# Removing the closing barrier of a one-core decode kernel, and splitting its last weight load

## The chip, the cores and the metric

The kernel runs on one core of one Trainium2 chip. The metric is device time in microseconds (us) for one execution. Each timed execution also gives a span: the time from the first to the last instruction that the profiler records. The time is longer than the span, by 1.27 to 1.95 us in the runs below, and that difference turns out to matter here; below it is called "time minus span".

The kernel has five engines at its disposal: TensorE (PE in the profile; PEld is its weight load), VectorE (DVE), ScalarE (ACT), GpSimd (POOL) and SyncE (SP), which here issues the store and all loads but two of 2 KB.

## The reference, cut to what matters

One token goes through a conditioned transformer block: a modulation vector from `c`, attention against a cache of 65,536 positions, and a gated feed-forward layer. Everything is a product of a vector with a matrix that is read once, so the time is mostly the time of reading 186 MB (on the page of the kernel before, loads are 75% of the chain that ended last).

```python
mod = (silu(c) @ w_mod).reshape(c.shape[0], 6, 1, -1)          # sa, ca, ga, sb, cb, gb
h = layernorm(x) * (1 + ca) + sa
x = x + ga * attention(h, k_cache, v_cache, wq, wo)             # 32 heads, 4 kv heads
h = layernorm(x) * (1 + cb) + sb
x = x + gb * ((gelu(h @ w_gate) * (h @ w_up)) @ w_down)         # w_down is 3584 x 1024
```

The change touches the last product (`w_down`, the down projection) and what follows the output store.

## The kernel before: the parts that matter

All loads are planned in one order and issued by SP. Each goes into one of ten buffers, and SP issues it once the buffer's previous user is done.

```python
def issue_ready():
    while issued[0] < len(loads):
        j = loads[issued[0]]
        if j.prev is not None:
            if j.prev.freed is None:
                return
            SP.wait(j.prev.freed)
        sp.dma_start(j.view, j.src).then_inc(j.tok[0], 16)
        issued[0] += 1
```

A product walks over its loads in order, waits for each whole load, and then issues its matmuls. With `nblk` = 8 the down projection has 8 matmuls for each 2 KB of row per partition.

```python
def matvec(bank, jobs, rhs, ready, nblk, pick=None, first=True):
    PE.wait(*ready)
    for (jb, view, k0, nk) in jobs:
        PE.wait(jb.tok)
        for kk in range(nk):
            for j in range(nblk):
                ins = pe.matmul(bank[:, j:j + 1], ..., rhs[:, k0 + kk:k0 + kk + 1], ...)
        tok = PE.done(ins)
        release(jb, tok)
    return tok
```

The down projection comes in three loads of 2 MB and two of 512 KB. Behind it stand two small VectorE operations, a transpose on TensorE, a cast and the store. The whole program is emitted inside a block, and leaving it is a barrier: in the profile of the kernel before, that line has a drain and a semaphore instruction of each of the five engines, the last ending at 442.67 us.

```python
while b < NBF:                                  # the last 1 MB: two loads of 512 KB
    for e in range(0, UE, 2):
        jb = plan_load(wd_v[:, b, e:e + 2, :], flat(2, D), next(tail))
        j_d.append((jb, jb.view, b * UE + e, 2))
    b += 1
...
    sp.dma_start(out[0, 0].rearrange("(j p) -> j p", p=P), y_row[:, :]).then_inc(out_sem, 16)
    sp.wait_ge(out_sem, 16)

with nc.Block() as block:
    @block.sync
    def _(sp_unused):
        emit_all()                              # emits on all engines
```

## Time and profile before

| | before |
|---|---|
| time, median of 3 runs | 444.28 us |
| span of the profiled run | 442.7 us |
| moved by loads, mean rate | 186 MB, 420 GB/s |
| TensorE busy | 76% of the span |
| chain that ended last | 75% loads |

These are lines of the page of the kernel before: the span, the busy share of TensorE, the load rate in 40 equal slices of the span, the sum over all load packets, and the shares of the chain that ended last.

```profile
span 442.7 us, 16779 instructions
PE 335.0 (76%) x7849; PEld 325.2 (73%) x7849; DVE 164.8 (37%) x282; ACT 143.1 (32%) x548; POOL 3.8 (1%) x21
...
GB/s 329 429 423 426 434 431 426 429 427 421 432 429 432 426 427 437 432 429 428 434 434 430 429 429 433 431 434 429 429 434 431 432 429 428 423 424 424 427 425 177
DMA packets 15392, 186.08 MB, mean 420 GB/s; under 512 B 1536, under 2 KB 1536, under 8 KB 3840
...
DMA 75%; PE 20%; issue 2%; DVE 1%; SPq 1%; ACT 1%
```

The rate is flat, 421 to 437 GB/s, from the second slice to the last but one. Only the two ends, at 329 and 177 GB/s, are not bound by the stream, and the change is at the second end.

The timeline of the kernel before shows that end. Columns: start, duration, engine, line, operation, output and inputs, count, and in brackets the idle time before and what ended it.

```profile
436.83 2.29 PE L316 MATMUL kt_ps<-u_col,slot 128*128 128x1 bf16 x80 [3.45 <-DMA slot<-in_B_w_down_dram]
...
439.28 0.58 PE L316 MATMUL kt_ps<-u_col,slot 128*128 128x1 bf16 x16 [0.15 <-DMA slot<-in_B_w_down_dram]
439.90 0.17 DVE L664 TENSOR_TENSOR t_dn<-kt_ps,mod_sb 128x8 f32<-128x8 f32 x1 [15.91 <-PE kt_ps L316]
...
441.04 0.37 SPq L672 DMA_DIRECT2D out_dram<-y_row  x1
```

TensorE does the last 2 MB load and the first 512 KB load in one go (80 matmuls), waits 0.15 us for the last 512 KB, and has 16 matmuls left. The store is issued at 441.04 us.

The barrier is on line 676. The view of that line lists each sequencer's instructions: engine, operation, count, duration in ns (least, median, most), and first and last start in us.

```profile
L676 POOLq EVENT_SEMAPHORE  x2: 17/17/17, 442.5 to 442.6; - x2
...
L676 ACTq DRAIN  x1: 256/256/256, 407.4 to 407.4; - x1
...
L676 SPq COMPARE_BRANCH  x1: 33/33/33, 442.3 to 442.3; - x1
L676 SPq DRAIN  x1: 7/7/7, 442.5 to 442.5; - x1
L676 SPq EVENT_SEMAPHORE  x1: 17/17/17, 442.6 to 442.6; - x1
...
L676 PEldq EVENT_SEMAPHORE  x1: 51/51/51, 442.6 to 442.6; - x1
```

SP's branch, at 442.29 in the instruction records, carries the wait for the store. SP's drain, GpSimd's gather and release, and the last semaphore waits of the engines follow; the last ends at 442.67. ScalarE drained at 407.4 already.

### The profile page before, as it was taken

Reading aid. Unit: us, or ns where it says so; the run is one execution under the profiler, and the core shown is the slowest. Engines: PE = TensorE matmul, PEld = TensorE weight load, DVE = VectorE, ACT = ScalarE, POOL = GpSimd, SP = SyncE. Lnnn points to the kernel's source line nnn. Section 1 sums busy time; section 2 is a strip of 40 time slices with the busy share of each in tenths; the row PEclk is TensorE's granted clock in tenths of the full one; section 3 lists DMA queues with packets and bytes.
Section 4 is the critical chain, followed back from the end, with each engine's and each line's share of the span. In section 5 each row is a group of like instructions: output and inputs, shape, how many; then the busy total and the mean of one; then the engine's idle time right before and its main releaser. Section 6 shows DMA issues by size and latency. Waiting matters only on the chain.

```text
span 442.7 us, 16779 instructions
## 1 busy us (share of the span) xinstructions
PE 335.0 (76%) x7849; PEld 325.2 (73%) x7849; DVE 164.8 (37%) x282; ACT 143.1 (32%) x548; POOL 3.8 (1%) x21
## 2 busy tenths in 40 slices
PE   1333468898979899989899988979898974654434
PEld 1333458898979899979799987969898964654434
DVE  1000046544536445544644644554544443210000
ACT  1000013444444333634533453543343562000000
POOL 2000000000000000000000000000000000000000
PEclk9999999867788956967955996895967785555555
DMA  8999999999999999999999999999999999999994
GB/s 329 429 423 426 434 431 426 429 427 421 432 429 432 426 427 437 432 429 428 434 434 430 429 429 433 431 434 429 429 434 431 432 429 428 423 424 424 427 425 177
DMA packets 15392, 186.08 MB, mean 420 GB/s; under 512 B 1536, under 2 KB 1536, under 8 KB 3840
## 3 DMA queue, kind: packets, MB, share of 16 engines
q1 hardware_dynamic: 15328, 185.61, 98.5%
q8 instruction: 25, 0.41, 0.3%
q14 instruction: 7, 0.06, 0.0%
q10 hardware_dynamic: 32, 0.00, 0.0%
HBM read 185.60 MB, written 0.00 MB: 419 GB/s over the span
## 4 chain that ended last, share of the span: by engine, by line
DMA 75%; PE 20%; issue 2%; DVE 1%; SPq 1%; ACT 1%
DMA slot<-in_A_v_cache_dram 55%; PE kt_ps L417 9%; DMA slot<-in_A_wq_dram 8%; DMA slot<-in_B_w_up_dram 6%; DMA slot<-in_B_w_down_dram 6%; PE b L481 5%; PE sc_ps L437 3%; PE kt_ps L316 1%; SPq L212 1%; PE b L461 1%; ACT p_sb L547 1%; PE b L451 1%; DVE kt_sb L612 0%; PE b L621 0%; DVE zs L597 0%
## 5 line engine op out<-in xcount | busy, mean ns | idle before, releaser
L417 PE MATMUL kt_ps<-ident,slot 128*128 128x128 bf16 x2048 | 171.9, 252 | 4.9 <-DMA slot<-in_A_k_cache_dram 3.0
L516 DVE COPY kt_sb<-kt_ps 128x2048 bf16<-128x2048 bf16 x96 | 117.5, 1225 | 100.0 <-PE kt_ps L417 99.7
L417 PEld LDWEIGHTS kt_ps<-ident,slot 128*128 128x128 bf16 x2048 | 148.6, 114 | 6.6 <-issue 4.2
L516 ACT ACTIVATE kt_sb<-kt_ps 128x2048 bf16<-128x2048 bf16 x32 | 60.1, 1878 | 217.7 <-PE kt_ps L417 217.7
L481 PE MATMUL b<-p_sb,slot 128*128 128x8 bf16 x2048 | 71.0, 167 | 29.5 <-DMA slot<-in_A_v_cache_dram 20.9
L481 PEld LDWEIGHTS b<-p_sb,slot 128*128 128x128 bf16 x2048 | 65.1, 100 | 32.2 <-DMA slot<-in_A_v_cache_dram 22.2
L547 ACT ACTIVATE p_sb<-sc_ps,mneg 128x64 bf16<-128x64 f32 x256 | 83.6, 560 | 5.7 <-DVE mneg L542 5.7
L547 ACT ACTIVATION_READ_ACCUMULATOR p_sb<-sc_ps,mneg 128x1 f32 x256 | 77.2, 364 | 0.0
L437 PE MATMUL sc_ps<-q_buf,kt_sb 128*128 128x8 bf16 x2048 | 67.4, 167 | 0.1
L437 PEld LDWEIGHTS sc_ps<-q_buf,kt_sb 128*128 128x128 bf16 x2048 | 65.1, 100 | 0.2 <-issue 0.2
L316 PE MATMUL kt_ps<-h_col,slot 128*128 128x1 bf16 x448 | 16.2, 172 | 16.9 <-DMA slot<-in_B_w_up_dram 9.1
L316 PEld LDWEIGHTS kt_ps<-h_col,slot 128*128 128x128 bf16 x448 | 15.6, 118 | 17.6 <-DMA slot<-in_B_w_up_dram 9.4
L316 PE MATMUL sc_ps<-s_col,slot 128*128 128x1 bf16 x384 | 11.5, 165 | 15.8 <-DMA slot<-in_w_mod_dram 15.8
L535 DVE TENSOR_REDUCE m_col<-sc_ps 128x8 f32<-128x512 f32 x32 | 21.8, 681 | 4.4 <-PE sc_ps L437 4.4
L316 PEld LDWEIGHTS sc_ps<-s_col,slot 128*128 128x128 bf16 x384 | 11.0, 105 | 16.4 <-DMA slot<-in_w_mod_dram 16.4
L540 DVE TENSOR_REDUCE mg<-b 8x1 f32<-8x128 f32 x32 | 8.9, 279 | 34.4 <-PE b L451 34.4
L316 PE MATMUL sc_ps<-h_col,slot 128*128 128x1 bf16 x256 | 7.4, 165 | 12.6 <-DMA slot<-in_A_wq_dram 12.6
L316 PEld LDWEIGHTS sc_ps<-h_col,slot 128*128 128x128 bf16 x256 | 7.1, 104 | 12.9 <-DMA slot<-in_A_wq_dram 9.3
L461 PE MATMUL b<-negi,mg 8*128 8x8 f32 x64 | 15.0, 304 | 0.4 <-DVE mg L540 0.4
L461 PEld LDWEIGHTS b<-negi,mg 8*128 8x128 f32 x64 | 12.0, 233 | 2.6 <-DVE mg L540 0.6
L316 PE MATMUL kt_ps<-u_col,slot 128*128 128x1 bf16 x224 | 6.6, 165 | 9.6 <-DMA slot<-in_B_w_down_dram 9.6
L316 PEld LDWEIGHTS kt_ps<-u_col,slot 128*128 128x128 bf16 x224 | 6.3, 104 | 9.9 <-DMA slot<-in_B_w_down_dram 6.8
(74 smaller groups left out, 63.2 us busy)
## 6 DMA issues: line engine op xcount, KB each, us to landing
slot<-in_A_k_cache_dram SPq DMA_DIRECT2D x32, 2048.0 KB, 29.6
slot<-in_A_v_cache_dram SPq DMA_DIRECT2D x32, 2048.0 KB, 33.2
slot<-in_w_mod_dram SPq DMA_DIRECT2D x8, 1536.0 KB, 19.0
slot<-in_A_wq_dram SPq DMA_DIRECT2D x4, 2048.0 KB, 37.0
slot<-in_A_wo_dram SPq DMA_DIRECT2D x4, 2048.0 KB, 34.7
slot<-in_B_w_gate_dram SPq DMA_DIRECT2D x4, 1792.0 KB, 39.4
slot<-in_B_w_up_dram SPq DMA_DIRECT2D x4, 1792.0 KB, 29.0
slot<-in_B_w_down_dram SPq DMA_DIRECT2D x3, 2048.0 KB, 30.4
```

The source lines that it names most:

```text
L212: sp.dma_start(j.view, j.src).then_inc(j.tok[0], 16)
L316: ins = pe.matmul(bank[:, j:j + 1], w, rhs[:, k0 + kk:k0 + kk + 1], start=first, stop=True, skip_group_check=True,)
L417: ins = pe.transpose(kt_ps[:, half * 2048 + t * P:half * 2048 + (t + 1) * P], j_k[i].view[:, b * TB + t, :], ident[:, :],)
L437: ins = pe.matmul(sc_ps[:, base + n * REP:base + (n + 1) * REP], kt_sb[:, j % 2, n, :], q_buf[:, j % SITES, :], start=True, stop=True,)
L451: ins = pe.transpose(b6[0:REP, 32:32 + P], m_col[:, j % 2, :], identf[:, :]) if emit else None
L461: ins = pe.matmul(b6[:, 256:256 + REP], mg8[:, j % 2:j % 2 + 1].to_broadcast([REP, P]), negi[:, :], start=True, stop=True,)
L481: ins = pe.matmul(b7[:, s * REP:(s + 1) * REP], j_v[j].view[:, n, :], p_sb[:, s, n, :], start=(n == 0), stop=(n == CH - 1),)
L516: ev[i % SITES][b].done(act.activation(dst, src, ACT.Copy) if E_ is AC else dve.tensor_copy(dst, src))
L535: m1[s].done(dve.tensor_reduce(m_col[:, j % 2, :].unsqueeze(2), scv, AX.X, ALU.max))
L540: m2[s].done(dve.tensor_reduce(mg8[:, j % 2:j % 2 + 1], b6[0:REP, 32:32 + P], AX.X, ALU.max))
L547: ins = act.activation(p_sb[:, s, :, h], scv[:, h, :], ACT.Exp, bias=mneg[:, j, h:h + 1], scale=scale, accum_out=z_all[:, j, h:h + 1],)
```

## The change

The intent is to save the barrier's own time behind the store, and to leave less TensorE work behind the last load to land. In this program the store depends on the last work of every other engine, so SP's wait for the store alone still comes after all of it.

```diff
-            for e in range(0, UE, 2):
-                jb = plan_load(wd_v[:, b, e:e + 2, :], flat(2, D), next(tail))
-                j_d.append((jb, jb.view, b * UE + e, 2))
+            for e, ne in ((0, 2), (2, 1), (3, 1)):
+                jb = plan_load(wd_v[:, b, e:e + ne, :], flat(ne, D), next(tail))
+                j_d.append((jb, jb.view, b * UE + e, ne))
             b += 1
@@ ...
-    with nc.Block() as block:
-        @block.sync
-        def _(sp_unused):
-            emit_all()
+    emit_all()
     return nc
```

## The prediction

> **What bounds the kernel now.** Loads. The page gives 186 MB at a mean of 420 GB/s in a span of 442.7 us, DMA engines 80% busy or more in every slice but the last, and DMA as 75% of the chain that ended last. TensorE is 76% busy. The change moves the same bytes, so only the end of the span is in play.
>
> **The tail now**, from the timeline and the instruction records (us from the span's start): 80 down-projection matmuls run from 436.83, starting 26.7 ns apart; the last starts at 438.96. TensorE then sits idle 0.15 us for the last 512 KB load (its last packet, a semaphore write, is at 438.86; TensorE resumes at 439.27). 16 matmuls end at 439.86; two DVE operations, a transpose and a cast end at 441.02. The store issues at 441.04 and SP's wait sees it at 442.29. Then come SP's branch out of the block, its drain at 442.45, GpSimd's gather and release at 442.48 and 442.56, and the other engines' last semaphore instructions, ending at 442.67.
>
> **Part 1, no closing barrier.** It removes everything after SP's wait: 442.67 - 442.31 = 0.36 us, all on the critical path. The other engines' drains go too, but ran long before (ScalarE's at 407.4, VectorE's at 440.7). The time on record is 1.6 us longer than the span, so something outside the program stays. [...] I expect no change in it.
>
> **Part 2, the split.** Packets of 4 KB take 159 ns, of 8 KB 309, of 16 KB 611: about 37 ns per KB plus some 10 ns each. Two of 2 KB should take about 170 ns where one of 4 KB took 159. Eight such pairs per engine make the last landing about 0.08 us later (estimate from those durations). [...] Against it, 8 matmuls instead of 16 remain behind the last landing: 8 x 26.7 ns = 0.21 us less. The first new load's 8 matmuls would run from 438.99 to 439.2, before the last landing is seen at about 439.35. Net gain: about 0.13 us. The extra load takes slot 5, freed when the gate product ends at about 406.5; SP would issue it at about 416.6, over 20 us before it is needed.
>
> **Sum.** 0.36 + 0.13 = 0.49 us, 0.11% of the time. Predicted 443.8 us, range 443.1 to 444.3. Chances: faster by over 2% 0.005, within 2% 0.99, slower by over 2% 0.005.
>
> **What would show it.** The span ends with SP's wait, about 1.25 us after the store's issue, near 442.2 us; TensorE's last group has 8 matmuls; 2 KB packets take near 85 ns; the store issues about 0.13 us earlier.
>
> **What would make it wrong.** [...] 2 KB packets could be slower than the larger ones suggest, so that the last load lands over 0.21 us later. Drift between runs (0.2 us in three) is as large as either part, so one pair of runs may not show the split.

## More of the kernel before

Kernels are compared only within the same rounds.

## The result

The changed kernel took 443.23 us (median of 5 runs, 443.03 to 443.25) against 444.28 us (5 runs, 444.04 to 444.35). The ratio is 0.9976, with a 95% interval of 0.9964 to 0.9988. Ratios here are the mean time of one kernel's fast runs over the mean of the other's of the same rounds, so not quite the ratio of the medians quoted. The gain is 1.05 us (0.24%). That is inside the predicted range but about twice the 0.49 us that the prediction worked out.

The lines of the changed kernel that answer to those above: the page, the timeline, and the line that now ends the program.

```profile
span 441.7 us, 16769 instructions
...
DMA packets 15537, 186.08 MB, mean 421 GB/s; under 512 B 1553, under 2 KB 1553, under 8 KB 3985
...
DMA 81%; PE 17%; issue 1%; SPq 1%; DVE 0%
```

```profile
436.37 2.86 PE L316 MATMUL kt_ps<-u_col,slot 128*128 128x1 bf16 x96 [3.02 <-DMA slot<-in_B_w_down_dram]
439.27 0.17 DVE L664 TENSOR_TENSOR t_dn<-kt_ps,mod_sb 128x8 f32<-128x8 f32 x1 [15.34 <-PE kt_ps L316]
...
440.41 0.37 SPq L672 DMA_DIRECT2D out_dram<-y_row  x1
```

```profile
L673 SPq EVENT_SEMAPHORE  x1: 17/17/17, 441.7 to 441.7; - x1
```

The program ends with SP's wait, 1.25 us after the store's issue, as predicted. In this pair of profiles the span is 0.99 us shorter: 0.36 us behind SP's wait, and 0.63 us because the store issues that much earlier (441.04 to 440.41). The prediction had 0.13 us for the second. Of the 0.63, the last landing, as TensorE sees it, accounts for 0.42 us (439.28 to 438.86 in the instruction records), and 8 matmuls fewer behind it for 0.21 us. The matmuls of the third 2 MB load already start 0.47 us earlier (436.83 to 436.37), before any load that the split touches is consumed. So the pair of profiles suggests that something other than the split moved the stream. That was the first thing to test.

### The profile page after: what moved, and what is told of

Read it like the earlier page. It is cut to its first block, busy times and chain, and to the rows that moved or that the text cites. A ratio compares the mean times of both kernels' runs of the same rounds, so it can differ in the third digit from the quotient of the medians.

```text
span 441.7 us, 16769 instructions
## 1 busy us (share of the span) xinstructions
PE 332.8 (75%) x7849; PEld 322.9 (73%) x7849; DVE 164.9 (37%) x282; ACT 143.1 (32%) x548; POOL 3.8 (1%) x21
## 4 chain that ended last, share of the span: by engine, by line
DMA 81%; PE 17%; issue 1%; SPq 1%; DVE 0%
DMA slot<-in_A_v_cache_dram 53%; DMA slot<-in_B_w_gate_dram 9%; PE kt_ps L417 9%; DMA slot<-in_A_k_cache_dram 8%; DMA slot<-in_B_w_down_dram 7%; DMA slot<-in_w_mod_dram 5%; PE b L481 4%; PE sc_ps L437 3%; PE kt_ps L316 1%; SPq L212 1%; PE b L451 0%; PE b L461 0%; DVE kt_sb L516 0%; PE b L668 0%; DVE y_row L670 0%
## 5 line engine op out<-in xcount | busy, mean ns | idle before, releaser
L417 PE MATMUL kt_ps<-ident,slot 128*128 128x128 bf16 x2048 | 170.1, 250 | 6.9 <-DMA slot<-in_A_k_cache_dram 3.2
```

The source lines that it names most:

```text
L417: ins = pe.transpose(kt_ps[:, half * 2048 + t * P:half * 2048 + (t + 1) * P], j_k[i].view[:, b * TB + t, :], ident[:, :],)
```

## The experiments

All runs are on the kernel before or on the changed kernel, with the edit named, and all returned correct results. Every call had 9 runs of the kernel before on the same chip. The table gives means; each kernel has 5 runs. "Gain" is the mean time, and the mean span, less those of the kernel before.

| run | closing barrier | last loads | time | span | time minus span | before: time minus span |
|---|---|---|---|---|---|---|
| e0 | yes | 512 + 512 KB | +0.01 | +0.02 | 1.83 | 1.84 |
| e1 | no | 512 + 512 KB | -0.95 | -0.44 | 1.34 | 1.84 |
| e2 | yes | 512 + 256 + 256 KB | -0.12 | -0.16 | 1.89 | 1.84 |
| e3 | no | 512 + 256 + 256 KB | -0.93 | -0.42 | 1.34 | 1.84 |
| f1 | no, all four others wait | 512 + 512 KB | -0.31 | -0.28 | 1.83 | 1.86 |
| f2 | no, ScalarE and GpSimd wait | 512 + 512 KB | -0.31 | -0.30 | 1.85 | 1.86 |
| f3 | no, TensorE and VectorE wait | 512 + 512 KB | -0.58 | -0.32 | 1.60 | 1.86 |
| f4 | no | 1 MB | -0.45 | +0.10 | 1.30 | 1.86 |
| g1 | no | 512 + 512 KB | -0.89 | -0.42 | 1.35 | 1.82 |
| g2 | no | 512 + 256 + 256 KB | -0.95 | -0.48 | 1.35 | 1.82 |
| g3 | no | as g2, one other load moved | +2.04 | +2.52 | 1.33 | 1.82 |
| h1 | no, ScalarE waits | 512 + 512 KB | -0.79 | -0.47 | 1.51 | 1.82 |

### The kernel before once more, and each part alone

e0 is the kernel before, unedited.

> The unchanged kernel, as a control: it gives the profile of the kernel before five more times. Theory C (chance: in the one profile shown of it a DMA engine started its loads 0.4 us late and stayed last to the end) expects spans of these runs mostly near 442.2 us, with 442.67 as an outlier. Theory S (the late engine belongs to the program as built) expects 442.6 us in all. Theory O (the barrier also costs time after the last instruction) expects time minus span near 1.6 us, against the 1.33 to 1.43 of the changed kernel's five runs.

e1 removes the barrier and keeps the loads:

```diff
-    with nc.Block() as block:
-        @block.sync
-        def _(sp_unused):
-            emit_all()
+    emit_all()
```

> No closing barrier, loads as before. The prediction's sum expects 0.36 us less than the kernel before, in the span and in the time. Theory O expects 0.36 us in the span and 0.2 us more outside it, 0.55 to 0.6 us in the time. Theory S[...] expects the last landing near 438.8 us as well and 0.9 us in the time.

e2 splits the load and keeps the block:

```diff
-            for e in range(0, UE, 2):
+            for e, ne in ((0, 2), (2, 1), (3, 1)):
```

> The split with the closing barrier kept. The prediction expects 0.13 us less, the last TensorE group 8 matmuls, the last landing 0.06 to 0.08 us later for the same start of the loads. A rival, that the split itself evens out the DMA engines, expects 0.5 us or more and the third 2 MB load of the down projection landing near 436.3 us instead of 436.8.

e3 is the changed kernel, unedited.

> Both parts, as changed, on this chip. If the parts add, its gain is that of e1 plus that of e2. The result on record says 1.05 us; the prediction says 0.49 us.

The medians were 443.95 us (e0), 442.94 (e1), 443.81 (e2) and 443.03 (e3), against 443.99 for the kernel before. The ratios were 1.0 (0.9987 to 1.0014), 0.9979 (0.9966 to 0.9993), 0.9997 (0.9983 to 1.0011) and 0.9979 (0.9965 to 0.9993). The barrier alone gives all of the gain; the split alone is not clear of noise.

The span of the first profile of before was an outlier, as theory C expected; theory S falls. In e0 the spans were 441.9 to 442.3 us, and in the 36 runs of before they were 442.0 to 442.5, with means of 442.10, 442.10, 442.38 and 442.39 on the four chips. None reached 442.67. In the first profile the last load engine to finish writes its semaphore 0.41 us behind the next one; in the profiles of e0, e1, f1, f2, f3, g1 and h1 it is 0.01 to 0.22 us. On the first three loads of the first profile that gap was already 0.32 to 0.39 us. The profile of e0 has the same program, but its last group starts 0.5 us earlier than in the first profile (438.78 against 439.28):

```profile
436.33 2.29 PE L316 MATMUL kt_ps<-u_col,slot 128*128 128x1 bf16 x80 [3.19 <-DMA slot<-in_B_w_down_dram]
...
438.78 0.58 PE L316 MATMUL kt_ps<-u_col,slot 128*128 128x1 bf16 x16 [0.16 <-DMA slot<-in_B_w_down_dram]
```

So most of the earlier landing in the first pair of profiles belonged to the run, not to the change.

With that outlier out of the way, the barrier's gain splits in two. The span loses 0.44 us in e1, near the 0.36 us of the barrier's instructions. The other half microsecond lies outside the span: time minus span falls from 1.83 us in e0 (1.75 to 1.93) to 1.34 us in e1 (1.30 to 1.37). This is theory O. The prediction had expected no change there.

### What the half microsecond outside the span is

Without the barrier, two things differ: the barrier's branch and drains are gone, and four engines reach their end before SP does (in the profile of the changed kernel GpSimd at 392.4 us, ScalarE at 407.5, TensorE at 440.1 and VectorE at 440.4, against 441.7 for SP). f1 keeps the first difference and undoes the second. It is e1 with four added waits and no barrier:

```diff
         sp.wait_ge(out_sem, 16)
+        pe.wait_ge(out_sem, 16)
+        dve.wait_ge(out_sem, 16)
+        act.wait_ge(out_sem, 16)
+        pool.wait_ge(out_sem, 16)
```

> No closing barrier, but TensorE, VectorE, ScalarE and GpSimd each wait at their end for the output store's semaphore, as SP does, so all five engines reach their end together. Theory E (in e1 about 0.5 us of the gain lies behind the last instruction, because four engines are done early and whatever ends a run on them overlaps the kernel) expects the span of e1, 441.7 us, but time minus span near 1.84 instead of 1.34, so a time near 443.5 us. Theory B (the barrier's own instructions, a branch and drains, cost that 0.5 us) expects time minus span to stay near 1.34 and the time near 443.0.

f2 adds only the waits of ScalarE and GpSimd, f3 only those of TensorE and VectorE.

> Only ScalarE and GpSimd wait for the store. If theory E holds and one of these two, which end earliest of all (407 and 391 us), sets the end, time minus span is near 1.84; if TensorE or VectorE does, it is 1.34.

> Only TensorE and VectorE wait for the store; without the wait they end about 1.2 to 1.9 us before SP. The mirror of f2: near 1.84 if one of these two sets the end, 1.34 if not, and something between if the cost adds up over the engines.

The views of f1's last lines show that it did what it was built for. All five engines end together, each with one wait and nothing else:

```profile
L673 SPq EVENT_SEMAPHORE  x1: 17/17/17, 441.9 to 441.9; - x1
L674 PEldq EVENT_SEMAPHORE  x1: 51/51/51, 441.9 to 441.9; - x1
L675 DVEq EVENT_SEMAPHORE  x1: 21/21/21, 441.9 to 441.9; - x1
L676 ACTq EVENT_SEMAPHORE  x1: 17/17/17, 441.9 to 441.9; - x1
L677 POOLq EVENT_SEMAPHORE  x1: 17/17/17, 441.9 to 441.9; - x1
```

Time minus span was 1.83 us in f1 (1.80 to 1.86), as with the barrier. Theory B, that the barrier's own instructions cost the half microsecond, falls: f1 has none of them. Theory E stands: what costs it is that engines with nothing left to do reach their end late. One thing stays untested: every engine that ends late in these runs ends with a semaphore wait of 17 to 51 ns, in the barrier as in f1, and no run gave an early engine such a wait that is already fulfilled. f2 gives the same 1.85 us (1.81 to 1.88) with two engines, and f3 1.60 us (1.56 to 1.62). The medians were 443.64, 443.68 and 443.42 us against 443.96, with ratios 0.9993 (0.9979 to 1.0006), 0.9993 (0.9979 to 1.0006) and 0.9987 (0.9973 to 1.0001).

Two engines cost as much as four, and another pair costs less, so the number of late engines alone does not explain it. Nor do the costs of the engines add up: above the 1.34 us of SP alone, f2 has 0.51 us and f3 0.26, together 0.77, and f1 with all four has 0.49. The last run, h1, lets only ScalarE wait:

```diff
         sp.wait_ge(out_sem, 16)
+        act.wait_ge(out_sem, 16)
```

> No closing barrier; of the four other engines only ScalarE waits for the store. f2 (ScalarE and GpSimd) gave time minus span 1.85 us, f3 (TensorE and VectorE) 1.60, none 1.34. If what follows the last instruction is a fixed stretch of each engine's own and the longest end counts, this run gives 1.85 if ScalarE has the long stretch, and 1.34 to 1.6 if it is GpSimd. If it is instead the number of late engines that counts, a single one should give less than the pair of f3, so below 1.6 as well; then only a value near 1.85 tells the two apart.

h1 gave 1.51 us (1.47 to 1.56), median 443.39 against 444.23 us, ratio 0.9982 (0.9969 to 0.9996). The reading that fits all these runs is that each engine has a stretch of its own behind its last instruction, by estimate from these means about 1.34 us for SP, 1.5 for ScalarE, 1.6 for the longer of TensorE and VectorE, and 1.85 for GpSimd, and that the engine that is through last counts. GpSimd's figure is by elimination, from f2 and h1 on two chips; it was not run alone, and neither were TensorE and VectorE, so this reading is argued and not shown; h1's value was, by its own expectation, not one that could decide. What fills the stretches cannot be seen, since the trace ends before them.

### The split

e2 gives -0.16 us in the span against the nine runs of before (-0.18 against e0), and e3 against e1 +0.02 us, so the split was still unclear. f4 turns its dose the other way, e1 with one load of 1 MB:

```diff
-            for e in range(0, UE, 2):
-                jb = plan_load(wd_v[:, b, e:e + 2, :], flat(2, D), next(tail))
-                j_d.append((jb, jb.view, b * UE + e, 2))
+            jb = plan_load(wd_v[:, b, :, :], flat(UE, D), next(tail))
+            j_d.append((jb, jb.view, b * UE, UE))
```

> No closing barrier, the last two 512 KB loads merged into one of 1 MB: the split's dose turned the other way. 32 matmuls remain behind the last landing instead of 16, at 26.7 ns: 0.43 us more, less at most 0.05 us for larger packets. The split's arithmetic in the prediction expects e1 plus about 0.4 us in span and time, 443.4 us; if the size of the last load hardly matters (as e3 against e1 seems to say, +0.02 us), about 443.0.

g1 and g2 are e1 and e3 again, side by side on another chip.

> The kernel of e1 a second time, for the split: e3 against e1 gave +0.02 us where e2 against e0 gave -0.16 us in the span, and f4 (1 MB) gave about +0.4 us. The arithmetic (16 matmuls at 26.7 ns behind the last landing against 8, less 0.03 us of longer stream) expects this run 0.15 to 0.2 us slower than g2 on average, and the same local stretch as before: 0.63 us from the last landing as TensorE sees it to the end of its last matmul. The rival, that the split is worth nothing without the barrier, expects the same time as g2.

> The changed kernel again, beside g1. Arithmetic: 0.15 to 0.2 us faster than g1, about 0.42 us from last landing to last matmul's end. Rival: equal to g1 within 0.05 us.

The 0.05 us for larger packets in the expectation of f4 and the 0.03 us of longer stream in that of g1 were estimates, with no source. The packet times (84 ns for 2 KB, 159 for 4 KB, 309 for 8 KB in the first two profiles) give an estimate of 0.07 us for either: 16 x 159 - 8 x 309 ns and 16 x 84 - 8 x 159 ns for each engine, taking the packets as spread evenly over 16 engines.

The profile of f4 has all 32 matmuls behind the last landing:

```profile
436.34 1.87 PE L315 MATMUL kt_ps<-u_col,slot 128*128 128x1 bf16 x64 [3.09 <-DMA slot<-in_B_w_down_dram]
438.76 1.01 PE L315 MATMUL kt_ps<-u_col,slot 128*128 128x1 bf16 x32 [0.56 <-DMA slot<-in_B_w_down_dram]
```

f4's median was 443.51 us against 443.96, ratio 0.999 (0.9976 to 1.0004). Its mean span, 442.20 us, is 0.40 us above the mean of f1, f2 and f3 on the same chip (441.80 us), which have the two 512 KB loads; the arithmetic said 0.43. So the work behind the last landing is on the critical path, at the price that the arithmetic sets.

g1's median was 443.41 us and g2's 443.29, against 444.20, ratios 0.9981 (0.9967 to 0.9995) and 0.9979 (0.9965 to 0.9992). The split is worth 0.06 us here in time and in span. The expected 0.15 to 0.2 us did not come, and "worth nothing" is not excluded. The instruction records show where the local gain went. These are starts in us, from the profiles of the two kernels:

```
                                    g1 (512 + 512)   g2 (512 + 256 + 256)
first matmul of the third 2 MB load        436.310                436.483
first matmul behind the last landing       438.758                439.064
last matmul of the down projection         439.181                439.273
```

Behind the last landing, 0.42 us became 0.21 us, as worked out. But the last landing came 0.31 us later in g2, and 0.17 us of that was there already when the third 2 MB load landed. Over all profiles with these loads except the outlier, TensorE sees the last landing at 438.79 us on average without the split (e0, e1, f1, f2, f3, g1, h1: 438.61 to 438.90) and at 438.94 with it (the changed kernel, e2, e3, g2: 438.86 to 439.06). The packets explain a part: those of 2 KB take 84 ns against 159 for 4 KB, which comes, by the estimate above, to 16 x 84 - 8 x 159 = 72 ns, some 0.07 us, for each engine, about half of the 0.15 us. The rest is smaller than the drift between runs, and these runs do not settle whether it belongs to the split.

### A last attempt, at the tail of the stream

The windows view of the kernel before shows that the load engines are only half used in the last microseconds. Columns: window, length, busy time of each engine (count of instructions), the granted clock, the load engines' busy share, GB/s.

```profile
433.00:434.00 1.00, 0.38 (x15) 0.30 (x12) 0.00 (x0) 0.00 (x0) 0.00 (x0) 0.50 0.92 385
...
436.00:437.00 1.00, 0.17 (x6) 0.17 (x7) 0.00 (x0) 0.00 (x0) 0.00 (x0) 0.50 0.52 213
437.00:438.00 1.00, 1.00 (x44) 1.00 (x41) 0.00 (x0) 0.00 (x0) 0.00 (x0) 0.50 0.47 193
```

In the profile of the kernel before, each of SP's 93 loads ends with 16 semaphore writes, and the two loads of 8 partitions (`c` and `x`) and the store, also of 8, with 8 each. They are read here as one write from each load engine that took part; the packet records carry no engine number. In every profile up to here, six of the last load's writes come 4.1 to 5.4 us before the last one, and eight in the last 1.2 us. A cause is inferred only: the first profile has 25 instruction packets of 16 KB, 24 of them before the last landing, of 879 to 1014 ns each. At the times of those 24, one load engine each falls back by about 1.5 us against the others (from the semaphore writes of successive loads), and at the end eight of 16 are 4.2 to 5.4 us behind the first. No run took these packets away. g3 is the changed kernel with 512 KB of the attention output weights sent as 16 loads of 8 partitions each, in the hope that they would use the eight early engines:

```diff
+        jo = j_o[-1][0]
+        k0, ks, cut = HQ - 8, 8, 6
+        jo.parts = [(jo.view[:, 0:cut, :], wo_v[:, k0:k0 + cut, :])]
+        for p0 in range(0, P, 8):
+            jo.parts.append((jo.view[p0:p0 + 8, cut:ks, :], wo_v[p0:p0 + 8, k0 + cut:k0 + ks, :]))
```

> The changed kernel with 512 KB of the attention output weights (the last 4 KB per partition of its last load) sent as 16 loads of 8 partitions, which should use 8 of the 16 DMA engines, instead of as part of a load over all 16. In every trace so far 8 engines finish their part of the last load 4.3 to 5 us after the leading ones. If the 8 engines used are the leading ones, the late ones carry 256 KB less, 32 KB each, about 1.2 us: last landing near 437.6 us, time about 442 us. If they are the late ones, the last landing is 1.2 us later and the time about 444.2 us. If it is a mixture, near 443 or later.

The 1.2 us is an estimate: 32 KB at the 37 ns per KB of the prediction's packet times.

It was slower: 446.17 us against 444.20, ratio 1.0045 (1.0032 to 1.0059). The last landing came at 442.1 us instead of 439.0 in g2. By the reading above, each of the 16 small loads did use eight engines: the profile has 128 more semaphore writes than that of g2 (1640 against 1512), eight for each added load. But most of the 3.1 us has another reason than the choice of engines. The windows of g2 and then of g3, for the 10 us in which the small loads land, show it:

```profile
380.00:385.00 5.00, 4.14 (x148) 4.04 (x149) 0.71 (x2) 0.00 (x0) 0.00 (x0) 0.50 1.01 428
385.00:390.00 5.00, 3.24 (x122) 3.16 (x120) 0.00 (x0) 0.00 (x0) 0.00 (x0) 0.50 0.99 415
```

```profile
380.00:385.00 5.00, 4.68 (x167) 4.58 (x167) 0.19 (x1) 0.00 (x0) 0.00 (x0) 0.50 1.00 310
385.00:390.00 5.00, 1.74 (x66) 1.65 (x63) 0.00 (x0) 0.00 (x0) 0.00 (x0) 0.50 1.01 319
```

The load engines are as busy as in g2, and the rate is a quarter lower: 1.07 MB less in 10 us, about 2.5 us of loading at 425 GB/s (an estimate from these four lines). Single packets took longer there: those of 4 KB 219 ns on average against 159 at the end of the same run, and those of 7 KB of the next loads 360 against 274 in the 10 us after it. Why is open. So g3 does not test cleanly which engines are early. About 0.6 us of the delay is left, between the 1.4 us gain that the expectation had for the early engines and the 1.2 us loss for the late ones, and the 16 semaphore writes of the last load no longer fall into an early and a late half: two come 6.3 to 6.5 us ahead of the last, eight 1.8 to 2.6 us ahead, and only two within 0.2 us of it. This looks like a mixture of early and late engines, but it is not shown. Which they were stays open, since the packet records carry no engine number.

## Why the prediction was right or wrong

- **What bounds the kernel, and that only the tail is in play: right.** The mean rate (420 and 421 GB/s) and the bytes did not change, and the chain stayed mostly loads (75% and 81%).
- **Part 1, inside the span: right.** 0.36 us was expected. Six kernels without the barrier and with the loads unchanged (e1, f1, f2, f3, g1, h1) have a mean span 0.28 to 0.47 us shorter than before, 0.37 us on average. The span ends with SP's wait, 1.25 us after the store's issue.
- **Part 1, outside the span: wrong, and this is the step that failed.** "I expect no change in it", the prediction says of what lies behind the kernel. Time minus span fell from 1.84 to 1.34 us, and f1 brought it back to 1.83 by making the four other engines wait. The prediction counted their early drains as costing nothing, because it read them inside the span. It also took 1.6 us for time minus span from a median time and one profile's span; taken run by run it is 1.74 to 1.94 in the 36 later runs.
- **Part 2, the split: the mechanism right, the net size not.** The matmuls behind the last landing went from 16 to 8, and f4 shows that 16 more cost 0.40 us. The 2 KB packets took 84 ns, where 85 was estimated; 84 ns is within some 6% of half a 4 KB packet's 159 ns. The net gain was expected at 0.13 us; measured were 0.12 (e2 against e0), -0.02 (e3 against e1) and 0.06 us (g2 against g1), 0.05 on average. The last landing came 0.15 us later on average where 0.08 was allowed; the packets account for 0.07 of it, and whether the rest belongs to the split is not settled.
- **The sum.** 0.36 + 0.50 + about 0.05 = 0.91 us; the two repeats of the changed kernel gained 0.93 and 0.95 us, and the result 1.05. That the measured time lies in the predicted range is in part luck: the range ran from no gain to 1.2 us, and half of the gain came from where the prediction expected none.
- **The span of 442.2 us and the store's issue 0.13 us earlier: missed in the pair of profiles** (441.7 us and 0.63 us), because the first profile of before was 0.3 to 0.6 us longer than that kernel's mean on the four later chips.

No version beat the changed kernel clearly. e1, without the split, is as fast within the noise.

## What to carry to other kernels

In this kernel an engine's end was part of the time, though nothing was left for it to do. So let engines that are done early end early, and close a kernel with a wait on the one engine that saw the store land, not with a barrier of all; here that was worth 0.37 us in the span and 0.5 us outside it, where no trace shows it. Form time minus span run by run before you decide that what lies outside the program is fixed. For effects below half a microsecond take several spans of the same kernel before reading a cause from two profiles: one unlucky profile here showed 0.4 us that the change did not make.
